# Where the first batch's x, its stage-A result and the expert weights live, and in which order they are asked for

## The chip, the cores and the metric

The kernel runs on one core of a Trainium2 chip. Its metric is the device time of one execution in microseconds (us). Engines are named as in the profile: PE is TensorE (PEld its weight loads), DVE is VectorE, ACT is ScalarE, POOL is GpSimd, SP is SyncE.

## What is computed

A Fourier layer and a layer of maxima over three products, on x of 8 batches x 3072 positions x 256 features:

```python
X = np.fft.rfft(x, axis=1)
Yr = Xr @ w_r - Xi @ w_i + b_r
Yi = Xr @ w_i + Xi @ w_r + b_i
Yr = np.sign(Yr) * np.maximum(np.abs(Yr) - 0.01, 0.0)      # Yi likewise
y = np.fft.irfft(Yr + 1j * Yi, n=3072, axis=1)
h = np.maximum(np.maximum(y @ w1, y @ w2), y @ w3)         # 256 -> 768
out = h @ w_out                                            # 768 -> 256
```

w1, w2, w3 and w_out come as 64-bit floats; the kernel reads their bits and makes two 16-bit parts of each.

## The kernel before

**Stages.** The transform of 3072 = 48 x 64 positions is done in two steps. Stage A (`stage_a`, TensorE line L408) multiplies eight chunks q of x by a table of 48 rows, copies the result (tile `pa`) out of PSUM on ScalarE (L410, two copies for each q, tiles `aq` or `zq`) and writes it to DRAM as `a_d` (L412, two DMAs, issued by ScalarE). Stages B, W and Q run over twelve k: `load_a` reads `a_d` back with other rows (tile `aj`; a k needs rows of all eight q), `stage_b` is the second step of the transform (`px`), `stage_w` the products with w_r and w_i (`py`), the bias and the soft threshold on VectorE (tile `uf`, lines L487, L548, L549), `finish_w` a maximum (L627), `stage_q` the first step of the inverse transform (`pz`), whose result goes to DRAM as `z_d`. Then `load_z` and `split_z` bring it back as two 16-bit halves `zh` (ScalarE) and `zl` (VectorE, L128), `inverse` does its second step (`pi`), and `up` and `down` are the expert network: for each of 8 column groups c and 6 slices f of 128 hidden features, 18 matmuls into `pu` and 9 into `pd`.

**Batches.** Batch 0 runs its transform alone, in 32-bit floats, ahead of everything. From then on the network of batch b runs with the transform of batch b + 1 in between: a sorted list `events` gives each step of that transform a place among the slots (c, f), and `run_until` calls what is due.

**Weights.** Eighteen parts of the expert weights (twelve of w1 to w3, 384 wide, and six of w_out, 256 wide) are loaded into tiles `rw` (14 buffers of tag `raw`), their largest value is taken (L276), and when all of a kind are there `scale` makes an exponent of it, with a small matmul `pt` (L199) between two reductions. `phases` then prepares a part in three steps, `exponent`, `combine` and `finish`, on VectorE and ScalarE; `pump` starts one part and moves those under way on by one step. `finish` writes the parts' halves into `wuh`, `wul`, `woh`, `wol`. The small weights w_r and w_i (tiles `wst`) are used as they are for batch 0 and split by `split_fft_weights`, called at f = 2 of the first column group.

**Order.** The instructions are not issued as written: a scheduler orders each engine's queue ahead of the run by place in the program and by when it expects an instruction's inputs, so that a later step may stand ahead of an earlier one on its engine. Within an engine the order is then fixed. `tc.issue_after(ins)` puts all that its block issues on the engine of `ins` behind `ins`.

**Places.** x of batch 0 goes alternately into tile `xq` (two buffers) and into tiles of tag `raw`; `aj` into two tags with two and three buffers; both are used again as soon as they have been read. x of batch 1, chunks 0 and 1 (q = 8 and 9) is loaded into `xq` during stages B to Q; their maxima (`mxx`, L394) are taken in `split_x`, ahead of `load_z`.

The start of the program's order of loads, which the change rewrites:

```python
    for q in range(3):
        load_x(q)
    for q in range(NCH):
        if q + 3 < NCH:
            load_x(q + 3)
        if q == 4:
            nc.sync.dma_start(out=id_sb, in_=ident)
            load_first_blocks(0)
            fft_weights = load_fft_weights()
        split_x(q)
        stage_a(q)
        if q in (5, 6, 7):
            load_units(w_up, up_units, 1)
```

## Time and profile before

| | |
|---|---|
| median of 3 runs | 2086.02 us (2083.11 to 2086.16) |
| profiled execution, its own time | 2082.1 us |
| its span | 2080.3 us |
| busy share of the span | PE 97%, PEld 67%, DVE 72%, ACT 47%, POOL 3% |
| mean granted clock of TensorE | 0.986 |
| moved by DMA | 165.16 MB, 79 GB/s on the mean |

The span runs from the first to the last instruction of the profile; the 1.8 us between it and the execution's own time lie around it. A busy TensorE is not one at its peak, since the ends of matmuls are modelled. The granted clock is 1.00 at 2.4 GHz and 0.50 at 1.2 GHz. Where the text speaks of a wait, the profile has inferred from semaphores what ended it.

### The profile page before, as it was taken

How to read it: one execution, taken by the hardware profiler on the slowest of the kernel's cores; microseconds unless marked ns; L12 is line 12 of the kernel's file. 1: busy time of each engine (PE TensorE's matmuls, PEld its weight loads, DVE VectorE, ACT ScalarE, POOL GpSimd, SP SyncE). 2: the span in 40 equal slices, each digit the busy share in tenths (PEclk: the TensorE clock that was granted, in tenths of full speed). 3: DMA queues.
4: the chain of work that ended last, by engine and by line, in shares of the span. 5: the costliest groups of instructions: out<-in, count | busy, mean ns of one | idle time of the engine just before them, and what ended most of it. 6: DMA issues, size and time to landing. Idle time of an engine off the chain costs nothing.

```text
span 2080.3 us, 39054 instructions
## 1 busy us (share of the span) xinstructions
PE 2022.4 (97%) x15603; PEld 1390.5 (67%) x15603; DVE 1494.4 (72%) x2951; ACT 967.9 (47%) x1929; POOL 71.2 (3%) x119
## 2 busy tenths in 40 slices
PE   5979999999999999999999999999999999999998
PEld 3746666676766666666676676666666677776666
DVE  1897888588866778668876688767887578865543
ACT  2355554455544545445554454444554445533333
POOL 0001000000000000000000000000000000000000
PEclk7989999999999999999999999999999999999999
DMA  8635231322213222132222232132221212111110
GB/s 270 191 97 154 71 90 59 100 72 77 72 57 103 74 85 67 59 99 80 74 65 83 75 89 72 59 100 72 82 77 52 72 56 67 41 42 37 33 29 23
DMA packets 116583, 165.16 MB, mean 79 GB/s; under 512 B 13137, under 2 KB 88914, under 8 KB 116306
## 3 DMA queue, kind: packets, MB, share of 16 engines
q1 hardware_dynamic: 54450, 87.15, 15.0%
q10 hardware_dynamic: 61952, 75.52, 11.8%
q8 instruction: 122, 2.00, 0.4%
q14 instruction: 59, 0.48, 0.1%
HBM read 87.13 MB, written 75.50 MB: 78 GB/s over the span
## 4 chain that ended last, share of the span: by engine, by line
PE 85%; DVE 7%; DMA 3%; ACT 2%; issue 2%; ACTq 0%; SPq 0%; POOL 0%; DVEq 0%; POOLq 0%
PE pu L133 17%; PE pu L135 17%; PE pu L134 17%; PE pd L135 6%; PE pd L133 6%; PE pd L134 5%; PE pa L408 3%; PE py L135 2%; PE py L134 2%; PE py L133 2%; DMA xq<-in_x_dram 2%; DVE u L591 1%; PE pi L133 1%; PE pi L135 1%; PE pi L134 1%
## 5 line engine op out<-in xcount | busy, mean ns | idle before, releaser
L133 PE MATMUL pu<-yh,wuh 128*128 128x384 f16 x2304 | 753.5, 327 | 0.4 <-ACT c L723 0.2
L134 PE MATMUL pu<-yl,wuh 128*128 128x384 f16 x2304 | 753.3, 327 | 0.0
L135 PE MATMUL pu<-yh,wul 128*128 128x384 f16 x2304 | 752.9, 327 | 0.0
L127 ACT ACTIVATE hh<-h 128x384 f16<-128x384 f32 x384 | 200.3, 522 | 516.2 <-DVE h L726 501.9
L724 DVE TENSOR_TENSOR c<-pu,c 128x384 f32<-128x384 f32 x384 | 212.8, 554 | 172.8 <-PE pu L135 102.5
L133 PEld LDWEIGHTS <-wuh 128*128 128x128 f16 x2304 | 225.9, 98 | 164.0 <-issue 35.5
L135 PEld LDWEIGHTS <-wul 128*128 128x128 f16 x2304 | 225.9, 98 | 149.1 <-issue 1.9
L135 PE MATMUL pd<-woh,hh 128*128 128x256 f16 x1152 | 313.4, 273 | 0.7 <-DVE hh L128 0.5
L133 PE MATMUL pd<-woh,hh 128*128 128x256 f16 x1152 | 313.8, 273 | 0.3 <-ACT hh L127 0.3
L134 PEld LDWEIGHTS <-wuh 128*128 128x128 f16 x2304 | 226.0, 98 | 131.5 <-issue 2.4
L134 PE MATMUL pd<-wol,hh 128*128 128x256 f16 x1152 | 313.7, 273 | 0.0
L128 DVE SCALAR_TENSOR_TENSOR hh<-h,hh 128x384 f16<-128x384 f32 x384 | 213.5, 556 | 115.9 <-ACT hh L127 111.8
L726 DVE TENSOR_TENSOR h<-pu,c 128x384 f32<-128x384 f32 x384 | 212.7, 554 | 47.4 <-PE pu L135 35.4
L723 ACT ACTIVATE c<-pu 128x384 f32<-128x384 f32 x384 | 186.2, 485 | 104.2 <-PE pu L135 98.2
L591 DVE SCALAR_TENSOR_TENSOR u<-py,s1x,cs 64x256 f32<-64x256 f32 x308 | 148.7, 483 | 44.9 <-ACT cs L602 40.1
L133 PE MATMUL py<-wch,tt 128*128 128x256 f16 x504 | 137.4, 273 | 0.0
L135 PE MATMUL py<-wch,tt 128*128 128x256 f16 x504 | 137.4, 273 | 0.0
L134 PE MATMUL py<-wcl,tt 128*128 128x256 f16 x504 | 137.4, 273 | 0.0
L133 PEld LDWEIGHTS <-hh 128*128 128x128 f16 x1152 | 112.7, 98 | 35.4 <-ACT hh L127 1.4
L134 PEld LDWEIGHTS <-hh 128*128 128x128 f16 x1152 | 112.7, 98 | 33.4
L135 PEld LDWEIGHTS <-hh 128*128 128x128 f16 x1152 | 112.7, 98 | 17.7 <-DVE hh L128 3.2
L749 ACT ACTIVATE o<-pd,s1u 128x256 f32<-128x256 f32 x192 | 83.2, 467 | 87.7 <-PE pd L135 42.2
(167 smaller groups left out, 2678.9 us busy)
## 6 DMA issues: line engine op xcount, KB each, us to landing
aj<-a_d SPq DMA_DIRECT2D x96, 256.0 KB, 2.9
z_d<-zs ACTq DMA_DIRECT2D x96, 256.0 KB, 2.2
zq<-z_d SPq DMA_DIRECT2D x128, 192.0 KB, 3.1
out_dram<-o ACTq DMA_DIRECT2D x192, 128.0 KB, 2.3
a_d<-aq ACTq DMA_DIRECT2D x124, 192.0 KB, 3.4
xq<-in_x_dram SPq DMA_DIRECT2D x120, 192.0 KB, 3.6
rw<-in_moe_w_dram SPq DMA_DIRECT2D x12, 384.0 KB, 6.8
xr<-in_x_dram SPq DMA_DIRECT2D x16, 96.0 KB, 3.8
```

Source lines behind the costliest of these rows:

```text
L127: nc.scalar.activation(out=hi, in_=src, func=AF.Copy, scale=scale)
L128: nc.vector.scalar_tensor_tensor(out=lo, in0=src, scalar=scale, in1=h, op0=ALU.mult, op1=ALU.subtract)
L133: nc.tensor.matmul(o, lh, rh, start=start, stop=False, **kw)
L134: nc.tensor.matmul(o, lh, rl, start=False, stop=False, **kw)
L135: nc.tensor.matmul(o, ll, rh, start=False, stop=stop, **kw)
L408: nc.tensor.matmul(pa[r][64 * c:64 * c + 64], fr[rows], xs[c][rows], start=True, stop=True)
L591: nc.vector.scalar_tensor_tensor(out=u[64 * c:64 * c + 64, j], in0=pk[r], scalar=inv[r], in1=c1[r], op0=ALU.mult, op1=ALU.add,)
L723: nc.scalar.activation(out=c1, in_=pu[0], func=AF.Copy)
L724: nc.vector.tensor_tensor(out=c1, in0=pu[1], in1=c1, op=ALU.max)
L726: nc.vector.tensor_tensor(out=h32, in0=pu[2], in1=c1, op=ALU.max)
L749: nc.scalar.activation(out=o, in_=pd[t], func=AF.Copy, scale=st[b, "su"][1])
```

## The change

- **Loads of x.** All eight chunks of batch 0's x are asked for first, with ten DMAs (two for chunk 0, two for chunk 1, then two for each pair of chunks); the identity, the first block of tables and the small weights are issued behind the last of them.
- **Places.** One tile `w_all` takes, one after the other, chunks 2 to 7 of x, all twelve `aj`, and the sixteen-bit halves of all expert weights.
- **Copies of stage A.** For batch 0 the second copy of each chunk goes to VectorE.
- **Loads of expert weights.** None during stage A; six are issued behind the third `aj`, the others as before by k.
- **Weight parts.** The subtraction and the addition in `finish` go from VectorE to GpSimd.
- **Behind stage Q.** `load_z` of batch 0 comes ahead of stage A of batch 1's chunks 0 and 1; their maxima, and the work of VectorE in `split_fft_weights`, are issued behind `zl`.

```diff
     def split_scaled(hi, lo, src, scale):
-        nc.vector.scalar_tensor_tensor(
+        return nc.vector.scalar_tensor_tensor(
...
-    wuh = const.tile([P, 3, KD, FF], F16, name="wuh")
-    wul = const.tile([P, 3, KD, FF], F16, name="wul")
-    woh = const.tile([P, NF, D], F16, name="woh")
-    wol = const.tile([P, NF, D], F16, name="wol")
+    HALF = FF // 2
+    w_all = const.tile([P, 2 * NJP * 2 * D], F16, name="w_all")
+    wup = w_all[:, 0:12 * FF].rearrange("p (v s i k w) -> p v s i k w", v=2, s=2, i=3, k=KD)
+    wdn = w_all[:, 12 * FF:].rearrange("p (f s d) -> p f s d", f=NF, s=2)
+    x_first = w_all.bitcast(F32).rearrange("p (q c w) -> p q c w", c=2, w=2 * D)
+    aj_first = w_all.bitcast(F32).rearrange("p (k d) -> p k d", d=D)
...
             def finish():
                 nc.scalar.activation(out=hi, in_=m, func=AF.Copy)
-                nc.vector.tensor_tensor(out=m, in0=m, in1=hi, op=ALU.subtract)
-                nc.vector.tensor_tensor(out=lo, in0=m, in1=r, op=ALU.add)
+                nc.gpsimd.tensor_tensor(out=m, in0=m, in1=hi, op=ALU.subtract)
+                nc.gpsimd.tensor_tensor(out=lo, in0=m, in1=r, op=ALU.add)
...
-    def load_x(q):
+    def load_x(q, count=1):
...
-            if q < NCH and q % 2:
-                pairs = [raw_tile("xr")[0:XR, 0:2 * D] for _ in range(2)]
-                for c, t in enumerate(pairs):
-                    for r in range(2):
-                        nc.sync.dma_start(out=t[64 * r:64 * r + N1], in_=xv[r, :, c])
+            if 2 <= q < NCH:
+                xq = x_first[:, q - 2:q - 2 + count]
             else:
-                xq = fft.tile([P, 2, 2 * D], F32, name="xq", bufs=2)
+                xq = fft.tile([P, 1, 2, 2 * D], F32, name="xq", bufs=2)
                 if b:
                     nc.gpsimd.memset(xq[32:64], 0.0)
-                for r in range(2):
-                    nc.sync.dma_start(out=xq[64 * r:64 * r + N1], in_=xv[r])
-                pairs = [xq[0:XR, c] for c in range(2)]
-        st["x", q] = pairs
+            for r in range(2):
+                dma = nc.sync.dma_start(
+                    out=xq[64 * r:64 * r + N1].rearrange("p q c w -> p (q c) w"),
+                    in_=xv[r, :, q4:q4 + count].rearrange("p q c w -> p (q c) w"),
+                )
+        if b == 0:
+            st["ld"] = dma
...
-    def split_x(q):
+    def largest_x(q):
...
         for r in range(2):
-            nc.scalar.activation(out=aq[:, r * 512:r * 512 + 512], in_=pa[r][0:XR], func=AF.Copy)
+            o = aq[:, r * 512:r * 512 + 512]
+            if b or r == 0:
+                nc.scalar.activation(out=o, in_=pa[r][0:XR], func=AF.Copy)
+            else:
+                nc.vector.tensor_copy(out=o, in_=pa[r][0:XR])
...
     def load_a(k):
-        first = ("vl", 3) if k < NJP and k % 5 > 1 else ("aj", 2)
-        st["a", k] = aj = fft.tile([P, 2, D], F32, name="aj", tag=first[0], bufs=first[1])
+        if k < NJP:
+            aj = aj_first[:, 2 * k:2 * k + 2]
+        else:
+            aj = fft.tile([P, 2, D], F32, name="aj", bufs=2)
+        st["a", k] = aj
...
-    for q in range(3):
-        load_x(q)
+    for q, count in ((0, 1), (1, 1), (2, 2), (4, 2), (6, 2)):
+        load_x(q, count)
+    with tc.issue_after(st["ld"].ins):
+        load_first_blocks(0)
+        fft_weights = load_fft_weights()
+        nc.sync.dma_start(out=id_sb, in_=ident)
     for q in range(NCH):
-        if q + 3 < NCH:
-            load_x(q + 3)
-        if q == 4:
-            nc.sync.dma_start(out=id_sb, in_=ident)
-            load_first_blocks(0)
-            fft_weights = load_fft_weights()
-        split_x(q)
         stage_a(q)
-        if q in (5, 6, 7):
-            load_units(w_up, up_units, 1)
-    for k in range(-3, NJP + 1):
+    for k in range(3):
+        load_a(k)
+    with tc.issue_after(st["ld"].ins):
+        load_units(w_up, up_units, 6)
+    for k in range(-1, NJP + 1):
         for fn, i in (
-            (load_a, k + 3), (stage_b, k + 1), (stage_w, k), (finish_w, k), (stage_q, k - 1),
+            (load_a, k + 4), (stage_b, k + 1), (stage_w, k), (finish_w, k), (stage_q, k - 1),
...
+    load_z(0, 0)
     for q in (NCH, NCH + 1):
-        split_x(q)
         stage_a(q)
-    load_z(0, 0)
     split_z(0)
     y = inverse(0, 0)
+    with tc.issue_after(st["zl"].ins):
+        for q in (NCH, NCH + 1):
+            largest_x(q)
...
                     if f == 2:
-                        split_fft_weights(fft_weights)
+                        with tc.issue_after(st["zl"].ins):
+                            split_fft_weights(fft_weights)
```

## Rows read from the trace of the kernel before

**Rows 1.** Busy time of every engine in four stretches of the span: up to the first px, from there to the last pz, from there to the first pu, and the rest (columns: stretch in us from the span's start; its length; busy us and count of instructions for PE, PEld, DVE, ACT and POOL; mean granted clock of TensorE; busy share of the DMA engines; GB/s).

```profile
0.00:39.54 39.54, 17.70 (x65) 6.15 (x65) 5.15 (x11) 10.59 (x18) 2.08 (x6) 0.71 0.80 238
39.54:114.30 74.76, 69.22 (x328) 55.00 (x328) 61.06 (x147) 27.89 (x57) 0.55 (x3) 0.95 0.65 206
114.30:128.50 14.20, 6.74 (x40) 3.67 (x40) 12.58 (x40) 6.39 (x11) 1.88 (x2) 0.55 0.66 167
128.50:2080.30 1951.80, 1928.70 (x15178) 1325.66 (x15175) 1415.61 (x2757) 923.01 (x1843) 66.66 (x108) 1.00 0.24 71
```

**Rows 2.** The chain of work that ended last, followed back and put in order of time, from 13 to 40 us (columns: start, duration, what).

```profile
19.46 4.96 DMA mb_all<-in_dft_ib_dram
...
26.86 5.83 DMA rw<-in_moe_w_dram
...
32.72 3.83 DMA a_d<-aq
...
36.62 2.87 DMA aj<-a_d
```

**Rows 3.** ScalarE and its queue of issued DMAs (ACTq) in order of time, 13 to 34 us (columns: start, duration, engine, line, operation, tiles, shapes, count; in brackets the idle time before it and what ended it).

```profile
26.04 0.88 ACTq L412 DMA_DIRECT2D a_d<-zq  x2
26.97 1.08 ACT L410 ACTIVATE aq<-pa 112x512 f32<-112x512 f32 x2 [4.60 <-DMA wst<-in_w_i_dram]
29.14 1.52 ACTq L412 DMA_DIRECT2D a_d<-aq  x2
30.71 0.60 ACT L410 ACTIVATE aq<-pa 112x512 f32<-112x512 f32 x1 [2.65 <-DMA qf<-in_dft_ib_dram]
```

**Rows 4.** Four short stretches, with the columns of rows 1; the last two figures of each line, DMA share and GB/s, are what is read here.

```profile
4.00:8.00 4.00, 3.48 (x14) 1.73 (x18) 0.00 (x0) 0.49 (x1) 0.00 (x0) 1.00 1.03 223
12.00:14.00 2.00, 2.00 (x11) 0.57 (x8) 0.00 (x0) 0.93 (x2) 0.54 (x1) 1.00 0.94 337
24.00:28.00 4.00, 0.00 (x0) 0.00 (x0) 2.03 (x4) 1.03 (x2) 0.00 (x0) 0.50 0.47 161
44.00:54.00 10.00, 10.00 (x47) 8.91 (x47) 4.89 (x9) 1.74 (x4) 0.00 (x0) 0.82 1.05 402
```

**Rows 5.** The same chain of work in order of time, from 0 to 60 us: three steps of TensorE at full clock.

```profile
49.67 0.43 PE py L483 x2
50.10 0.89 PE px L456 x8
...
54.01 0.86 PE pz L495 x2
```

**Rows 6.** The stretch from 58 to 114 us, with the columns of rows 1.

```profile
58.00:114.00 56.00, 51.17 (x250) 40.04 (x248) 51.27 (x128) 23.81 (x48) 0.55 (x3) 1.00 0.54 155
```

**Rows 7.** The same chain in order of time, from 94 to 129 us.

```profile
96.50 1.86 DVE mxx L394 x3
...
98.68 0.59 DVE mxx L394
...
105.31 0.34 DVE wol L324
...
112.47 0.61 DVE uf L549
...
116.42 4.94 DMA xq<-in_x_dram
121.49 0.69 DVE mxx L394
...
122.91 0.47 DVE rw L323
...
125.06 0.59 DVE mxx L394
125.65 1.20 DVE zl L128
```

**Rows 8.** All engines in order of time, 117 to 123.5 us, with the columns of rows 3: the load of zq (SPq, the queue of SyncE) and the first instruction that reads it.

```profile
117.51 1.34 SPq L683 DMA_DIRECT2D zq<-z_d  x2
...
122.96 1.15 ACT L127 ACTIVATE zh<-zq,s0u 96x1024 f16<-96x1024 f32 x1 [1.58 <-DMA zq<-z_d]
```

**Rows 9.** What TensorE's matmuls waited for between 39.6 and 128.5 us (columns: engine and line, what it waited for, us in total, times, longest).

```profile
PE px L456 <- DMA aj<-a_d: 16.1, 1, 16.1
...
PE pt L199 <- DVE col L197: 2.7, 2, 2.2
PE pz L498 <- DVE uf L549: 2.3, 1, 2.3
```

**Rows 10.** VectorE's groups of instructions between 58 and 114 us, one for each line and shape (columns: line, engine, operation, tiles, shapes, count; busy us, mean ns of one; idle time before them).

```profile
L549 DVE TENSOR_TENSOR uf<-uf,t 128x512 f32<-128x512 f32 x10 | 6.8, 685 | 0.0
...
L323 DVE TENSOR_TENSOR rw<-rw,wuh 128x384 f32<-128x384 f32 x6 | 3.3, 551 | 0.0
...
L323 DVE TENSOR_TENSOR rw<-rw,woh 128x256 f32<-128x256 f32 x3 | 1.3, 418 | 0.0
```

**Rows 11.** GpSimd's groups over the whole span, with the columns of rows 10.

```profile
L532 POOL TENSOR_SCALAR tt<-tt 128x256 f16<-128x256 f16 x14 | 10.3, 736 | 314.0 <-ACT tt L127 255.3 <-DVE hh L128 58.6
L540 POOL COPY ts<-tt 128x256 f16<-128x256 f16 x14 | 5.5, 396 | 0.9
```

**Rows 12.** DMA issues by tile over the whole span (columns: tiles, queue, operation, count, KB each, median us from issue to landing).

```profile
zq<-z_d SPq DMA_DIRECT2D x128, 192.0 KB, 3.1
```

More of the change, by code (lines that the diff above doesn't have):

```diff
@@ L329, in fourier_maxout_kernel @@
     out_v2 = w_out.bitcast(U32)
-    HALF = FF // 2
     w_up = Weights("u", [
-        (wuh[:, i, kd, v:v + HALF], wul[:, i, kd, v:v + HALF],
-         up_v[i][kd * P:(kd + 1) * P, 2 * v:2 * v + 2 * HALF])
-        for v in range(0, FF, HALF) for i in range(3) for kd in range(KD)
+        (wup[:, v, 0, i, kd], wup[:, v, 1, i, kd],
+         up_v[i][kd * P:(kd + 1) * P, 2 * v * HALF:2 * (v + 1) * HALF])
+        for v in range(2) for i in range(3) for kd in range(KD)
     ])
     w_dn = Weights("d", [
-        (woh[:, f], wol[:, f], out_v2[f * P:(f + 1) * P]) for f in range(NF)
+        (wdn[:, f, 0], wdn[:, f, 1], out_v2[f * P:(f + 1) * P]) for f in range(NF)
     ])
@@ L368, in rows_of @@
         return v[2 * k:2 * k + 2].rearrange("j p d -> p j d")
[L371 removed]
+    def load_x(q, count=1):
         b, q4 = divmod(q, NCH)
[L373 removed]
+        xv = x[b].rearrange("(n1 q c r n) d -> r n1 q c (n d)", n1=N1, c=2, r=2, n=2)
         with tc.issue_after(st["ld"].ins) if q >= NCH + 2 else nullcontext():
[L375 to L379 removed]
+            if 2 <= q < NCH:
+                xq = x_first[:, q - 2:q - 2 + count]
             else:
[L381 removed]
+                xq = fft.tile([P, 1, 2, 2 * D], F32, name="xq", bufs=2)
                 if b:
                     nc.gpsimd.memset(xq[32:64], 0.0)
[L384 to L398 removed]
+            for r in range(2):
[5 more added lines that the diff above has]
+            st["ld"] = dma
+        for i in range(count):
+            st["x", q + i] = [xq[0:XR, i, c] for c in range(2)]
+    def largest_x(q):
+        b, q4 = divmod(q, NCH)
+        for i, xp in enumerate(st["x", q]):
+            nc.vector.tensor_reduce(
+                out=batch(b, "x")[0:XR, 2 * q4 + i:2 * q4 + i + 1], in_=xp, axis=AX.X,
+                op=ALU.max, apply_absolute_value=True,
+            )
     def stage_a(q):
@@ L409, in stage_a @@
         for r in range(2):
-            nc.scalar.activation(out=aq[:, r * 512:r * 512 + 512], in_=pa[r][0:XR], func=AF.Copy)
+            o = aq[:, r * 512:r * 512 + 512]
[3 more added lines that the diff above has]
+                nc.vector.tensor_copy(out=o, in_=pa[r][0:XR])
         for c in range(2):
+            n0 = 8 * q4 + 4 * c
             nc.scalar.dma_start(
-                out=batch(b, "a")[:, 8 * q4 + 4 * c:8 * q4 + 4 * c + 4, :],
+                out=batch(b, "a")[:, n0:n0 + 4, :],
                 in_=aq[64 * c:64 * c + N1].rearrange("p (n d) -> p n d", n=NQ),
@@ L691, in split_z @@
         zl = fft.tile([96, NQ, D], F16, name="zl", bufs=1)
-        split_scaled(*(t.rearrange("p n d -> p (n d)") for t in (zh, zl)), st["zq"], st[b, "su"][0][0:96])
+        st["zl"] = split_scaled(
+            *(t.rearrange("p n d -> p (n d)") for t in (zh, zl)), st["zq"], st[b, "su"][0][0:96]
+        )
         st["z"] = zh, zl
@@ L717, in up @@
                 mm3(
-                    p[:, 0:NT], wuh[:, i, kd, f * P:(f + 1) * P], wul[:, i, kd, f * P:(f + 1) * P],
-                    y[0][:, kd], y[1][:, kd], start=kd == 0, stop=kd == KD - 1,
+                    p[:, 0:NT],
+                    *(wup[:, f // 3, s, i, kd, f % 3 * P:f % 3 * P + P] for s in range(2)), y[0][:, kd], y[1][:, kd], start=kd == 0, stop=kd == KD - 1,
                 )
@@ L742, in down @@
             mm3(
-                pd[t], lh, ll, woh[:, f], wol[:, f], start=f == 0 and t != 1,
+                pd[t], lh, ll, wdn[:, f, 0], wdn[:, f, 1], start=f == 0 and t != 1,
                 stop=f == NF - 1 and t != 0, skip_group_check=t < 2,
@@ L795, in fourier_maxout_kernel @@
         with tc.issue_after(st["ld"].ins):
-            if k in (-2, 1, 4):
-                load_first_blocks(k // 3 + 2)
+            if k in (-1, 1, 4):
+                load_first_blocks((k + 5) // 3)
             load_units(w_up, up_units, 2)
```

15 lines of the change are left out of this document (2 added, 13 removed).

## The prediction, made before the changed kernel ran

> **What bounds the kernel now.** I read the busy time by stages first [rows 1]. The last 1951.8 us, from the first matmul of the expert network on, keep TensorE busy for 1928.7 us at full clock; nothing in the diff takes matmuls out of that stretch, so what the change can move lies in the 128.5 us ahead of it. There the rows show three stages. Until 39.54 us TensorE works for 17.7 us only: x comes in, stage A runs, its result goes to DRAM. Then 74.76 us of the first batch's stages B, W and Q. Then 14.2 us from the last pz to the first pu, with TensorE busy for 6.74 us and a mean clock of 0.55.
>
> In the first stage I followed the chain [rows 2]. Behind the x loads it runs over the first table (4.96 us), over the first expert weights rw (5.83 us), to the last write of a_d (3.83 us) and the first load of aj (2.87 us). The ScalarE rows [rows 3] show why loads of tables stand on a path of writes: the write of a_d issued at 26.04 and the copies behind it start only when a wst load has landed (4.60 us idle), the next when qf has (2.65 us idle). Those copies read neither tile, so it is the writes' issue that waits for earlier transfers of the other queue, and it holds ScalarE's copies up behind it. The transfers [rows 4]: x alone moves 223 GB/s with the queues full (1.03), x and a_d together 337, and from 24 to 28 us there is a hole (share 0.47).
>
> In the second stage the reader is to see that TensorE has no time to give until late. Per k the chain has 0.89 us for px, sixteen py in pairs of 0.43, and 0.86 for pz [rows 5], so 5.2 us, times 12 is 62 us. Until about 96 us that is back to back. VectorE is busy for 51.27 of 56 us there [rows 6] and falls behind at the end: four maxima of batch 1's x (1.86 + 0.59 us) stand in its queue at 96.5, and the last uf reaches TensorE at 113.1 [rows 7].
>
> In the third stage [rows 7, 8] zq is asked for at 117.51, zh starts at 122.96, but zl not before 125.65, since two maxima that wait for a late xq (4.94 us) stand ahead of it.
>
> **The change part by part.** The base is the profiled execution, 2082.1 us with a span of 2080.3.
>
> *x first, tables behind, copies on two engines.* 24 DMAs for batch 0's x become 10, none waits for a buffer any more, and the bytes are the same. Eight chunks of 393 kB are 3.15 MB; at 223 GB/s 14.1 us. As much again for a_d, at 337 GB/s or more, is 9.3 us at most; twelve tables (1.3 MB) at the same rate take 4 us. That is 27.4 us of a full queue from 2 us on, so the last a_d can't land before about 27 to 29 us (before: 36.55, where the aj load starts). Three rw loads (1.2 MB, 3.5 us) that stood ahead of the last writes now stand behind three aj loads. So the bound from below is 28 + 2.87 = 31, a gain of 8.5. From above: the twelve tables are now asked for directly behind x, while the writes of a_d still wait for earlier transfers of the other queue, now bigger ones. If the second a_d waits for the last x (about 18 us), seven chunks are left; each has about 0.6 us of copy on ScalarE and two writes issued (0.88 to 1.52 us for two [rows 3]), 1.5 to 2.1 us, together 10.5 to 15, and 3.8 to land: 32 to 37, the gain is between 4.5 and nothing. The half of the copies that goes to VectorE costs about 0.6 us each (as on ScalarE) while VectorE is idle, and shortens this chain. I take 31.5, so first px at 34.5: **5 us gained** (0 to 8.5). At half clock TensorE starts into stage B as before, so that ramp neither costs nor pays.
>
> *aj kept in the weights' place.* TensorE waits for no aj once stage B runs (the one wait, 16.1 us, is the first px) [rows 9], so more buffers are worth nothing there. Their price is that weight parts may be written only when the px that read that place are over; the parts are finished several k later, and I put it at nothing. SP issues aj, rw and tables in the old order but for three aj in front; TensorE takes its fourth aj three px and two times sixteen py after the first, 9.6 us, and 3.3 MB lie ahead of it, 8.3 us at the 400 GB/s that aj and rw bring from 44 us on [rows 4]: covered by 1.3 us, and by more while the clock is at half.
>
> *GpSimd finishes the weight parts.* Two VectorE instructions per part leave. Start to start they cost 0.47 us (384 wide) and 0.34 us (256 wide) [rows 7], so nine parts (six and three [rows 10]) give back 6 x 0.94 + 3 x 0.68 = 7.7 us of the 51.27, and the moved maxima another 2.45. What GpSimd needs for two inputs no row shows. Its copy of 256 elements takes 396 ns, its scalar form 736 [rows 11]; two copies' worth would be 0.8, so for 384 elements between 0.6 and 1.2 us; I take 1.1 (the scalar form's rate) and 0.74 for 256. Nine parts are 17.6 us on an idle engine. If that hid completely, TensorE would get back at most its waits behind VectorE [rows 9]: 2.7 for pt and 2.3 for pz, 5 us. If GpSimd and VectorE exclude each other, VectorE's 41.1 us grow by up to 17.6 to 58.7, which is 7.4 more than today. Between these, with half of it colliding, VectorE has 50 us, and the maxima are away from the place where they cost most: **2 us gained** (-7.4 to 5).
>
> Here a page speaks against the change. The Trainium skill, "SBUF — State Buffer", section "Who interferes with whom", has the two engines share one port pair as an exclusive lock: a VectorE instruction with two SBUF inputs, or in a two-port mode, and a GpSimd instruction that reads SBUF wait for each other in full. No row here shows it: GpSimd's rows before are copies, fills and a scalar form. By the rule the sum would go to its lower end, as far as L309, L316, L317 and L549 (two SBUF inputs each, as L549's row shows [rows 10]) meet GpSimd.
>
> *z ahead of batch 1's x.* zl then waits for zh and zq alone. zq was asked for at 117.51 and its median landing is 3.1 us [rows 12], against some 5 here beside xq and a_d. With zq at 121, zl ends at 122.3 instead of 126.85. A write of a_d still runs beside it, and one GpSimd instruction may be in the way: **4 us gained** (2 to 5). Late is then x of chunk 10, which waits for the maxima behind zl; its matmuls have slot 3 among the events, three f later, so that is hidden.
>
> *The start of the network.* The split of the small weights also moves behind zl: its reduces and its four pt matmuls ran in idle gaps and now run among the first pu. Nine more parts on GpSimd have to be done by the fourth f, three f of 1951.8/384 = 5.1 us on: 17.6 us of GpSimd against 15, begun before. I count **0.5 us lost** (-1 to 4).
>
> Sum: 5 + 2 + 4 - 0.5 = 10.5 us. Span 2069.8, own time 2071.6. The median of the runs stands 3.9 us above the profiled execution (2086.02), so I forecast **2075.5 us**. About 0.2%, 4 us, is what a measurement can tell from no change.
>
> **The rivals.** *Tables in the way*: stage A ends as late as now, because tables and writes wait for each other as [rows 3] show, only earlier placed. Then 0 to 1 instead of 5: 2080. For it speaks that table loads aren't taken away, against it that rw is.
>
> *The port*, the one on the other side: every GpSimd instruction holds VectorE up. Stages B to Q take 7.4 us more instead of 2 less, and the second nine parts hold VectorE, full at that point, up by another 17.6 - 7.7 = 10 us, of which TensorE's reserve takes perhaps half. 5 + 4 - 7.4 - 5 = -3.4, so 2089, and 2083 to 2092 with the gains' own bounds. It decides once the net hold in both stretches passes some 9 us.
>
> *Everything hides*: stage A ends at its transfer bound (8.5), TensorE's waits behind VectorE go (4.5), zl 4.5: 17.5 gained, 2068.5.
>
> **How the numbers follow.** Forecast 0.47; everything hides 0.17; tables 0.17; the port 0.19, half of it near no change, half slower. Faster: 0.47 + 0.17 + most of the tables' case (0.13) = 0.77; the same 0.04 + 0.09 = 0.13; slower 0.10. The range holds the first three and the near half of the port: 2065 to 2086.
>
> **What would show it.** The first px between 31 and 37 us; copies of stage A without waits for wst or qf; TensorE without a wait for VectorE's col around the dn maxima; VectorE's two-input instructions longer than 0.55 us or with gaps beside GpSimd's if the port rules; zl right behind zh; first pu near 118 us, and from there 1952 us as now. Wrong it would be if the stretch behind the first pu grew, or if TensorE waited within stages B to Q.

## The result and the profile after

The changed kernel takes 2095.69 us (median of 4 runs, 2094.10 to 2097.70), the kernel before 2085.56 (4 runs); the ratio is 1.0051, 95% interval 1.0034 to 1.0069. By the medians that is 10.1 us slower where 10.5 us faster was forecast, and outside the range. The profiled execution took 2096.82 us with a span of 2095.0.

The same four stretches as in [rows 1], of the changed kernel:

```profile
0.00:40.21 40.21, 21.49 (x64) 5.52 (x65) 5.53 (x8) 6.36 (x10) 2.09 (x6) 1.00 0.85 204
40.21:124.43 84.22, 72.57 (x327) 57.44 (x328) 63.70 (x139) 29.19 (x60) 23.18 (x25) 0.93 0.61 197
124.43:136.83 12.40, 6.82 (x35) 3.04 (x36) 8.23 (x26) 5.92 (x10) 3.97 (x5) 0.50 0.47 133
136.83:2095.00 1958.17, 1930.36 (x15179) 1326.37 (x15177) 1417.72 (x2752) 921.39 (x1841) 76.39 (x120) 1.00 0.25 71
```

Against [rows 1] the first stretch is 0.7 us longer, the second 9.5, the third 1.8 shorter, the last 6.4 longer: 14.7 us of span, some more than the medians show. In the second stretch TensorE is busy for 72.57 us instead of 69.22, so 6.1 of the 9.5 us are idle time and 3.4 are matmuls that took longer, at a mean granted clock of 0.93 against 0.95. The 1.00 in the first row is no reading: the trace of this run has no record of the clock before 45.1 us.

**Stage A.** The chain of the changed kernel from 9 to 41 us, in order of time:

```profile
9.82 0.37 ACTq L417
...
10.23 7.41 DMA a_d<-aq
...
18.17 6.91 DMA a_d<-zq
...
28.87 3.79 DMA bias<-in_b_i_dram
...
33.51 3.75 DMA a_d<-aq
...
37.34 2.73 DMA w_all<-a_d
```

A write of a_d issued into the burst of x takes 7.41 us to land, the next on the chain 6.91; [rows 2] has 3.83 for one. SyncE's queue tells the other half:

```profile
3.06 15.36 SPq L383 DMA_DIRECT2D w_all<-in_x_dram  x6
18.47 0.94 SPq L767 DMA_DIRECT2D mb_all<-in_dft_ib_dram  x1
```

The six loads of x behind the first four are not all issued by 6 us; it takes until 18.4, the tables follow at 18.5, and the small weights at 25. Their places are free, and they read no a_d; what their issue waited for (SyncE, 0 to 42 us; us in total, times, longest) is all the same

```profile
SPq L383 <- DMA a_d<-aq: 9.8, 2, 9.2
```

In the trace the DMAs of SyncE and ScalarE take eight completion semaphores in turn, and none is issued before the one that had its semaphore last has landed: the load of x issued at 17.26 us follows the landing of ScalarE's first write of a_d at 17.24. What ScalarE waited for meanwhile (8 to 41 us), and the last of these waits in order of time:

```profile
...
ACT aq L412 <- DMA a_d<-aq: 4.9, 1, 4.9
ACT aq L412 <- DMA a_d<-zq: 4.3, 1, 4.3
ACT zq L412 <- DMA a_d<-zq: 4.2, 1, 4.2
```

```profile
26.96 3.02 ACTq L417 DMA_DIRECT2D a_d<-zq  x2
30.07 1.08 ACT L412 ACTIVATE aq<-pa 112x512 f32<-112x512 f32 x2 [4.30 <-DMA a_d<-zq]
```

The copies' waits for wst and qf of [rows 3] are gone, and 13.4 us of waits for a write of a_d stand in their place. In 9.1 of them a copy needs the buffer (two aq, one zq) whose write is still on its way. In the other 4.3 an aq is named as held up by a write of zq, which frees no aq: there the copy stands in ScalarE's queue behind the issue of zq's two writes, which takes 3.02 us because the second waits for an earlier write to land.

**Stages B to Q.** VectorE's and GpSimd's groups in the changed kernel (columns as [rows 10]; VectorE from 58 to 125 us, GpSimd from 50 to 200 us):

```profile
L555 DVE TENSOR_TENSOR uf<-uf,t 128x512 f32<-128x512 f32 x10 | 7.6, 755 | 0.0
L311 DVE SCALAR_TENSOR_TENSOR xl<-rw,xl 128x384 uint32<-128x384 uint32 x9 | 7.0, 779 | 0.8 <-ACT xl L307 0.8
L633 DVE TENSOR_REDUCE mxu<-uf 128x1 f32<-128x512 f32 x10 | 6.8, 677 | 0.0
...
L278 DVE TENSOR_REDUCE mwd<-rw 128x1 f32<-128x256 f32 x6 | 2.5, 417 | 8.3 <-DMA rw<-in_moe_w_out_dram 8.3
```

```profile
L325 POOL TENSOR_TENSOR rw<-rw,w_all 128x384 f32<-128x384 f32 x12 | 13.4, 1113 | 89.1 <-DMA w_all<-a_d 57.5 <-ACT w_all L324 31.5
L326 POOL TENSOR_TENSOR w_all<-rw 128x384 f16<-128x384 f32 x12 | 10.8, 899 | 1.9 <-PE px L462 1.1
```

L555 is L549 of [rows 10], 685 ns there, and L311 is this line of the kernel before (58 to 125 us):

```profile
L309 DVE SCALAR_TENSOR_TENSOR xl<-rw,xl 128x384 uint32<-128x384 uint32 x9 | 5.0, 552 | 0.7 <-ACT xl L305 0.7
```

The maxima mwd (L278) wait 8.3 us for loads of w_out; the raw buffers these need are freed by GpSimd's finish, and each of the six loads is issued within 0.1 us behind the end of an L326. That this makes the whole wait is not shown: with the finish on GpSimd alone (e2) it is 1.0 us. The reader sees the longer instructions one by one where the two engines meet (start, duration):

```profile
116.71 0.67 DVE L633 TENSOR_REDUCE mxu<-uf 128x1 f32<-128x512 f32 x1
117.31 1.24 DVE L311 SCALAR_TENSOR_TENSOR xl<-rw,xl 128x384 uint32<-128x384 uint32 x1
...
121.04 0.55 DVE L319 SCALAR_TENSOR_TENSOR rw<-rw,xl 128x384 f32<-128x384 uint32 x1
121.51 1.40 DVE L555 TENSOR_TENSOR uf<-uf,t 128x512 f32<-128x512 f32 x1
```

```profile
117.22 0.91 POOL L325 TENSOR_TENSOR rw<-rw,w_all 128x384 f32<-128x384 f32 x1
118.21 1.02 POOL L326 TENSOR_TENSOR w_all<-rw 128x384 f16<-128x384 f32 x1
121.45 0.91 POOL L325 TENSOR_TENSOR rw<-rw,w_all 128x384 f32<-128x384 f32 x1 [2.23 <-ACT w_all L324]
```

L311 beside L325 takes 1.24 us and L555 beside the next 1.40, each about its own time plus most of GpSimd's; L319, with GpSimd idle until near its end, 0.55.

**Behind the first pu.** The first eight f of the network (up to the start of the ninth hh on ScalarE), first in the kernel before and then in the changed one, and two stretches of the latter (columns as [rows 1]):

```profile
128.50:178.80 50.30, 49.60 (x308) 25.85 (x306) 43.50 (x107) 27.08 (x56) 5.71 (x6) 0.96 0.41 119
136.60:195.30 58.70, 53.47 (x312) 26.90 (x311) 46.17 (x103) 25.69 (x54) 15.57 (x19) 0.88 0.43 115
145.00:165.00 20.00, 14.91 (x91) 8.00 (x93) 20.00 (x56) 10.21 (x22) 7.10 (x9) 0.99 0.08 20
164.60:174.80 10.20, 10.20 (x30) 2.94 (x27) 7.84 (x17) 4.05 (x9) 1.89 (x2) 0.50 0.58 155
```

From 145 to 165 us VectorE is busy without a gap and TensorE for 14.9 of 20 us: the network starts on a VectorE that has a backlog. Behind that TensorE runs at 1.2 GHz for 10 us; the kernel before, where it stood for 0.7 us in all, stays at 2.4 GHz there. So the backlog is paid twice: of the 8.4 us that the first eight f grew by, 4.5 are idle time of TensorE, and 3.9 are matmuls, about as many, that took longer.

### The profile page after: what moved, and what is told of

It reads as the page before. It is cut to its first block, busy times and chain, and to the rows that moved or that the text cites. A ratio compares the mean times of both kernels' runs of the same rounds, so it can differ in the third digit from the quotient of the medians.

```text
span 2095.0 us, 39066 instructions
## 1 busy us (share of the span) xinstructions
PE 2031.2 (97%) x15603; PEld 1392.4 (66%) x15603; DVE 1495.2 (71%) x2923; ACT 962.9 (46%) x1921; POOL 105.6 (5%) x155
## 3 DMA queue, kind: packets, MB, share of 16 engines
q1 hardware_dynamic: 54226, 87.15, 15.5%
## 4 chain that ended last, share of the span: by engine, by line
PE 87%; DVE 5%; DMA 3%; ACT 2%; issue 2%; POOL 0%; ACTq 0%; SPq 0%; DVEq 0%; POOLq 0%
PE pu L133 17%; PE pu L135 17%; PE pu L134 17%; PE pd L135 6%; PE pd L133 6%; PE pd L134 6%; PE pa L408 3%; PE py L133 2%; PE py L135 2%; PE py L134 2%; DMA xq<-in_x_dram 2%; PE pi L133 1%; DVE u L597 1%; PE pi L135 1%; PE pi L134 1%
## 5 line engine op out<-in xcount | busy, mean ns | idle before, releaser
L133 PE MATMUL pu<-yh,w_all 128*128 128x384 f16 x2304 | 753.3, 327 | 1.7 <-DVE c L732 1.5
L134 PE MATMUL pu<-yl,w_all 128*128 128x384 f16 x2304 | 752.8, 327 | 0.0
L135 PE MATMUL pu<-yh,w_all 128*128 128x384 f16 x2304 | 752.6, 327 | 0.0
L133 PEld LDWEIGHTS <-w_all 128*128 128x128 f16 x2304 | 225.8, 98 | 164.7 <-issue 35.9
L135 PEld LDWEIGHTS <-w_all 128*128 128x128 f16 x2304 | 225.9, 98 | 149.1 <-issue 1.7
L135 PE MATMUL pd<-w_all,hh 128*128 128x256 f16 x1152 | 313.7, 273 | 1.7 <-DVE hh L128 1.6
L133 PE MATMUL pd<-w_all,hh 128*128 128x256 f16 x1152 | 314.2, 273 | 0.8 <-ACT hh L127 0.8
L134 PEld LDWEIGHTS <-w_all 128*128 128x128 f16 x2304 | 226.0, 98 | 132.9 <-issue 3.9
L134 PE MATMUL pd<-w_all,hh 128*128 128x256 f16 x1152 | 314.2, 273 | 0.0
L757 ACT ACTIVATE o<-pd,s1u 128x256 f32<-128x256 f32 x192 | 83.3, 467 | 89.8 <-PE pd L135 44.7
```

The source lines that it names most:

```text
L133: nc.tensor.matmul(o, lh, rh, start=start, stop=False, **kw)
L134: nc.tensor.matmul(o, lh, rl, start=False, stop=False, **kw)
L135: nc.tensor.matmul(o, ll, rh, start=False, stop=stop, **kw)
L757: nc.scalar.activation(out=o, in_=pd[t], func=AF.Copy, scale=st[b, "su"][1])
```

## The experiments

All times are compared with runs of the kernel before on the same chip. The lengths of stretches are from each kernel's profiled execution: start of the first px; from there to the start of batch 0's last pz; from there to the first pu; from there to the start of the ninth hh (the first eight f); the rest. A profiled execution varies by itself: eight kernels with the stage A of before have their first px between 37.4 and 40.3 us, six with its stages B to Q (before, e3, e5, e6, e13, e17) reach the last pz 73.0 to 75.6 us later, and eight with its start of the network (before, e4, e7, e9, e10, e11, e17, e18) need 49.1 to 50.7 us for the first eight f. A difference within these spans shows nothing. The profiled executions of e4, e5, e7 and e11 were 2.7, 6.3, 3.4 and 2.9 us above their medians, that of e9 3.3 below.

| kernel | ratio to before, 95% | first px | to last pz | to first pu | first eight f | rest |
|---|---|---|---|---|---|---|
| before | 1 | 39.5 | 74.4 | 14.6 | 50.3 | 1901.5 |
| changed | 1.0051 (1.0034 to 1.0069) | 40.2 | 83.6 | 12.8 | 58.7 | 1899.7 |
| e1 loads and z | 1.0074 (1.0062 to 1.0086) | 39.2 | 80.7 | 12.6 | 63.2 | 1901.9 |
| e2 GpSimd alone | 1.0038 (1.0026 to 1.0050) | 38.8 | 83.1 | 18.1 | 48.1 | 1900.5 |
| e3 z alone | 1.0047 (1.0035 to 1.0059) | 38.9 | 73.6 | 12.1 | 64.6 | 1903.2 |
| e4 loads alone | 1.0025 (1.0014 to 1.0036) | 40.7 | 80.1 | 14.8 | 50.5 | 1903.2 |
| e5 z, split free | 1.0000 (0.9991 to 1.0009) | 40.3 | 74.8 | 12.4 | 57.7 | 1901.5 |
| e6 split late | 1.0044 (1.0031 to 1.0057) | 39.8 | 75.6 | 15.4 | 58.3 | 1902.3 |
| e7 e4, 4 zs | 1.0015 (1.0006 to 1.0024) | 39.7 | 78.2 | 15.3 | 50.7 | 1902.7 |
| e8 idle GpSimd | 1.0044 (1.0032 to 1.0057) | 38.9 | 77.2 | 14.6 | 57.6 | 1900.9 |
| e9 e7, 4 aq | 0.9995 (0.9986 to 1.0004) | 36.7 | 74.7 | 15.1 | 49.8 | 1897.6 |
| e10 e7, x in 8 | 1.0010 (1.0001 to 1.0019) | 39.3 | 75.1 | 14.0 | 50.7 | 1900.9 |
| e11 e9, tables late | 1.0015 (1.0006 to 1.0024) | 35.8 | 80.8 | 15.4 | 49.1 | 1902.5 |
| e12 GpSimd, half | 1.0003 (0.9994 to 1.0012) | 37.4 | 72.8 | 14.5 | 51.3 | 1900.6 |
| e13 batch 1 later | 1.0014 (1.0004 to 1.0023) | 38.5 | 73.0 | 16.3 | 41.2 | 1914.3 |
| e14 changed, later | 1.0070 (1.0058 to 1.0082) | 39.8 | 80.7 | 12.8 | 47.4 | 1912.5 |
| e15 e9, x8, z, later | 1.0027 (1.0016 to 1.0039) | 38.2 | 76.2 | 13.1 | 44.7 | 1911.6 |
| e16 e15 without z | 1.0025 (1.0013 to 1.0037) | 38.1 | 76.0 | 17.2 | 40.7 | 1914.3 |
| e17 before, 4 aq | 1.0003 (0.9992 to 1.0015) | 38.2 | 73.0 | 15.3 | 50.1 | 1904.6 |
| e18 e9, zq first | 1.0004 (0.9993 to 1.0014) | 37.6 | 74.9 | 15.5 | 50.5 | 1903.4 |

**The change taken apart, e1 to e4.** The first theory after the result was that GpSimd's finish alone is to blame (G).

e1: the changed kernel with the finish on VectorE.

```diff
-                nc.gpsimd.tensor_tensor(out=m, in0=m, in1=hi, op=ALU.subtract)
-                nc.gpsimd.tensor_tensor(out=lo, in0=m, in1=r, op=ALU.add)
+                nc.vector.tensor_tensor(out=m, in0=m, in1=hi, op=ALU.subtract)
+                nc.vector.tensor_tensor(out=lo, in0=m, in1=r, op=ALU.add)
```

> The changed kernel with the two instructions that finish a weight part given back to VectorE; loads, places and z stay changed. Theory G (GpSimd's finish is what costs: it stretches VectorE's instructions and frees the raw buffers late): the 9.4 us that the stretch from first to last pz grew by and the 6.4 us behind the first pu both go, 2095.7 - 15.8 = 2080. Rival P (the places: parts that wait until aj and x have left them): it stays within 3 us of 2095.7. Rival Z (the weights' split pushed behind the first pu by the z move): the 6.4 us stay, the 9.4 go, 2086.

2098.05 us against 2081.96. It is not faster than the changed kernel, so G, by which GpSimd alone is to blame, falls.

e2: the kernel before with those two lines the other way round.

> The kernel before with the finish on GpSimd and nothing else. Theory G: 2085.6 plus 12 to 16, 2098 to 2102. Rival P or Z: between 2083 and 2087, since VectorE has less to do and nothing else is touched.

2090.18 us, 8 us lost: 8.7 to the last pz, 3.5 to the first pu, and 2.2 won back in the first eight f. Both theories missed: G wanted 12 to 16, the others no loss.

e3: the kernel before with z loaded first, the maxima and the split behind zl.

```diff
+    load_z(0, 0)
     for q in (NCH, NCH + 1):
         split_x(q)
         stage_a(q)
-    load_z(0, 0)
     split_z(0)
     y = inverse(0, 0)
+    with tc.issue_after(st["zl"].ins):
+        for q in (NCH, NCH + 1):
+            largest_x(q)
...
-                        split_fft_weights(fft_weights)
+                        with tc.issue_after(st["zl"].ins):
+                            split_fft_weights(fft_weights)
```

> The kernel before with z loaded first and the two maxima and the weights' split behind zl, and nothing else. Theory G: the stretch from last pz to first pu shrinks by 1.8 us (as in the changed kernel) to 4 us (as forecast), the rest as before: 2081.5 to 2084. Rival Z: the network loses 3 to 6 us: 2086 to 2090.

2092.23 us. The z stage is 2.5 us shorter, the first eight f 14.3 longer: more than rival Z had put there.

e4: e1 without the z part.

> The loads and places alone: x asked for first, x and aj kept in the weights' place, tables behind x, half of the first batch's copies on VectorE; the finish on VectorE and z as before. Theory G: stage A 0.7 us later as in the changed kernel, nothing else: 2085 to 2087. Rival P: 2092 to 2096. If the forecast's 5 us are merely hidden by GpSimd's trouble: 2081.

2088.49 us, between the times of G and P: 5.7 us lost between the first px and the last pz, the stretch that rival P means, though not for its reason (e7). Each of the three parts is slower by itself: 0.25% for loads and places, 0.47% for z, 0.38% for GpSimd. Loads and z add up (0.72% against e1's 0.74%). With GpSimd all three come to 0.51% instead of 1.1%: beside the other two its finish doesn't cost 8 us more. By the ratios it gives 5 back, but the intervals of e1 and the changed kernel overlap, so that it gives anything is not shown. The first eight f show some of it: 63.2 in e1, 58.7 in the changed kernel. Why the three add up to so little was not tried.

**The split behind zl, e5 and e6.** e5 is e3 with the split taken up whenever it can be; e6 is the kernel before with nothing but the split held behind zl.

```diff
                     if f == 2:
-                        split_fft_weights(fft_weights)
+                        with tc.issue_after(st["zl"].ins):
+                            split_fft_weights(fft_weights)
```

> z alone as in e3, but the split of the small weights may again be taken up before zl. Theory S (the split, held behind zl, is what fills VectorE in the first f of the network): the first eight f come back from 64.6 to about 50 us, the 2.5 us of the z stage stay won: 2078 to 2080 against 2082 before. Rival M (VectorE's backlog, maxima and weight parts, is merely moved from the idle z stage into the network, whatever is named): 2088 to 2092, no better than e3.

> The kernel before with the split of the small weights held behind zl; z and the maxima stay where they were. Theory S: the first eight f take 8 to 14 us longer: 2088 to 2094. Rival M: 2081 to 2084, since the order of z and the maxima is untouched.

e5 took 2082.22 us, e6 2091.90. So z and the maxima without the split cost nothing and bring nothing, neither the 2 to 4 us of theory S nor the loss of rival M; the split held late is 9 us by itself, and it is what e3 lost by. Where it went is in the maxima of the small weights, of the kernel before and of e6 (count, min/median/max ns, first and last start in us):

```profile
L233 DVE TENSOR_REDUCE mxc<-wst x2: 686/686/687, 25.3 to 26.3; 128x1 f32<-128x512 f32 x2
```

```profile
L233 DVE TENSOR_REDUCE mxc<-wst x2: 678/679/680, 150.5 to 151.9; 128x1 f32<-128x512 f32 x2
L243 DVE TENSOR_TENSOR wst<-wst x2: 414/414/415, 152.5 to 152.9; 128x256 f32<-128x256 f32 x2
```

In the kernel before they ran at 25 us (the maximum of the bias at 34.4, ql at 36.1), on a VectorE that had nothing to do in stage A. Behind zl they run at 150 us, on the engine that TensorE waits for there; two mxc, two subtractions, the maximum of the bias and ql are 3.3 us. Busy times of e6 (columns as [rows 1]) and the longest wait of its ScalarE from 136 to 160 us:

```profile
136.00:144.00 8.00, 5.92 (x39) 3.62 (x37) 8.00 (x22) 4.58 (x9) 0.00 (x0) 1.00 0.01 3
144.00:152.00 8.00, 6.93 (x43) 3.85 (x42) 7.97 (x23) 2.80 (x7) 0.00 (x0) 1.00 0.00 0
152.00:160.00 8.00, 6.36 (x40) 3.15 (x41) 8.00 (x31) 3.49 (x9) 0.95 (x1) 1.00 0.18 49
```

```profile
ACT wch L127 <- DVE sc L215: 4.5, 1, 4.5
```

VectorE is full, and ScalarE stands for 4.5 us at wch, up to 156.9, for the scale that comes out of the late maxima; in the kernel before its longest wait for the split there is 0.6 us. Work and wait are not a sum, since ScalarE waits while VectorE does that work. Nor are they the whole 8.0 us that the first eight f grew by: TensorE lacks 2.1 us from 136 to 144 already, ahead of the first late maximum, where the kernel before lacks 0.7:

```profile
136.00:144.00 8.00, 7.30 (x44) 3.82 (x42) 8.00 (x24) 4.57 (x9) 0.00 (x0) 1.00 0.00 0
```

Holding the split also changed the order in which VectorE took the weight parts; what that costs was not tried apart. Nearly all of e6's growth is idle time of TensorE (7.8 us against 0.7, busy for 50.5 against 49.6). In e3, which grew by 14.3, it is 9.4 us of idle time, and 55.2 us busy at a mean granted clock of 0.84.

**Stage A and the loads, e7 and e9 to e11.** ScalarE in e4 (columns as [rows 3]):

```profile
64.79 0.38 ACTq L653 DMA_DIRECT2D z_d<-zs  x1
...
68.94 0.60 ACT L307 ACTIVATE xl<-xh,bwu 128x384 uint32<-128x384 uint32 x1
74.48 0.60 ACT L652 ACTIVATE zs<-pz 128x512 f32<-128x512 f32 x1 [4.94 <-DMA z_d<-zs]
...
75.58 0.54 ACT L324 ACTIVATE w_all<-rw 128x384 f16<-128x384 f32 x1 [0.50 <-ACT zs L652]
```

With no buffer to wait for, four aj and the table ga_sb are asked for between 61 and 64 us, and one write of z_d, issued at 64.79, lands 9.6 us later. ScalarE stands for its zs buffer, and the weight part behind it waits too. e7 gives zs four buffers.

```diff
-        zs = fft.tile([P, 2, D], F32, name="zs")
+        zs = fft.tile([P, 2, D], F32, name="zs", bufs=4)
```

> e4 with four buffers for zs instead of two, so that ScalarE's copy need not wait for a late write of z_d. Theory Q (aj no longer waits for a buffer, so more loads stand in the queues; one z_d write takes 9.6 us beside them, ScalarE stands for 4.9 us at zs, and the weight parts behind it come late): the stretch from first px to last pz goes from 80.1 back to 75 to 76, the time to 2083 to 2085. Rival P (weight parts wait until x and aj have left their place): 80 us and 2088 stay.

2084.94 us, as expected, but the stretch to the last pz came down to 78.2 only, 1.9 us where 4 to 5 were expected. That is less than such stretches vary, and e7's profiled execution was a long one: e10, whose program is the same from the first px on, has 75.1. ScalarE's wait for z_d is gone; what theory Q is worth lies between these. e9 has four aq as well:

```diff
-        return fft.tile([XR, NQ * D], F32, name=name, bufs=1 if name == "zq" else 2)
+        return fft.tile([XR, NQ * D], F32, name=name, bufs=1 if name == "zq" else 4)
```

> e7 with four buffers for aq instead of two. Theory buffers (stage A's copies wait for the write of the chunk that had the buffer before: 4.44, 4.17 and 4.25 us in e7, since a write beside the burst of x takes 7 us to land): most of these waits go, the first px comes at 32 to 36 instead of 39.7 us, the time is 2079 to 2082. Rival queue (the transfers themselves are the limit): the first px stays at 38 to 40, 2084 to 2086.

2079.03 us against 2079.11 before. The intervals of e9 and e7 don't meet. The first px is 3.0 us earlier than in e7, at 36.7 where 32 to 36 was expected, and the stretch to the last pz back at 74.7. The five kernels with x first and two aq have their first px at 39.2 to 40.7 (changed, e1, e4, e7, e14), e18 with e9's stage A at 37.6, so 2 to 3 us of this are the buffers'. That makes their theory right in its result; but ScalarE still waits for writes (8 to 34 us):

```profile
ACT aq L412 <- DMA a_d<-zq: 10.9, 2, 6.9
...
ACT zq L412 <- DMA a_d<-zq: 0.4, 1, 0.4
```

11.3 us of waits are left of e7's 12.9, 6.9 of them ahead of the last two chunks. But for 0.4 us they are not for buffers, since a write of zq frees no aq: the copies stand in ScalarE's queue behind the issue of writes, as above. How the buffers bring their gain is thus not shown in full.

e10, x in eight DMAs instead of ten:

```diff
-    for q, count in ((0, 1), (1, 1), (2, 2), (4, 2), (6, 2)):
+    for q, count in ((0, 1), (1, 1), (2, 3), (5, 3)):
```

> e7 with batch 0's x in eight DMAs (1, 1, 3 and 3 chunks) instead of ten. Theory lanes (the last two x loads are issued at 17.15 and 18.07 us only, because each waits for a write of a_d that was issued in its turn before it): all x is asked for by 8 us, the stall of SP's queue is gone, the first px comes at 36 to 38, 2081 to 2084. Rival buffers: x was not what the copies waited for, and the writes behind a longer burst land later still: first px 39 to 42, 2084 to 2087.

2081.81 us against 2079.11, so not clearly faster than e7 by the ratios. All x is asked for by 11.8 instead of 18.4 us, and the first px moves by 0.4: the late issues of x are not what stage A waits for.

e11, the small tables behind three aj:

```diff
         load_first_blocks(0)
-        fft_weights = load_fft_weights()
-        nc.sync.dma_start(out=id_sb, in_=ident)
...
+    with tc.issue_after(st["ld"].ins):
+        fft_weights = load_fft_weights()
+        nc.sync.dma_start(out=id_sb, in_=ident)
```

> e9 with the small weights, the bias, qf and the identity asked for behind the first three aj instead of behind x. If tables still stand in the way of the writes (the writes of chunks 5 to 7 wait for bias and qf between 26 and 34 us in e7), the first px comes 1 to 4 us earlier than in e9 and the time falls by as much; the price is that the bias and qf come late for the first uf and pz, at most 2 us. If not: as e9 within 1 us.

2082.45 us. Stage A ends 0.9 us earlier, less than it varies, and 6 us are lost behind it, more than the price expected, and ScalarE's row names it (36 to 60 us):

```profile
ACT tf L467 <- DMA wst<-in_w_i_dram: 11.2, 1, 11.2
```

e17 gives the kernel before four aq and nothing else.

> The kernel before with four buffers for aq instead of two, and nothing else. If the three microseconds that e9 won in stage A are the buffers' alone, the first px comes 2 to 3 us earlier here too and the time is 2 to 4 us below before. If they need x asked for first (in the kernel before the copies lose 7.3 us to issues that wait for tables and some 4 us to buffers): the first px moves by less than 1 us and the time stays within 2 us of before.

2081.43 us against 2080.82: no change. So the buffers are worth something only to x asked for first, and x asked for first is worth nothing measurable over the kernel before even with them.

**GpSimd and VectorE, e8 and e12.** e8 leaves VectorE's work alone and adds two GpSimd instructions for each part whose result nobody reads.

```diff
                 nc.vector.tensor_tensor(out=lo, in0=m, in1=r, op=ALU.add)
+                s = fft.tile([P, 384], F32, name="scratch", bufs=1)[:, 0:width]
+                nc.gpsimd.tensor_tensor(out=s, in0=hi, in1=hi, op=ALU.subtract)
+                nc.gpsimd.tensor_tensor(out=s, in0=s, in1=s, op=ALU.add)
```

> The kernel before, VectorE's finish untouched, and beside it two GpSimd two-input instructions per part on a scratch tile whose result nobody reads: work added, none taken. Theory port (GpSimd and VectorE hold each other up): VectorE's two-input instructions stretch, the stretch from first px to last pz grows by half or more of e2's 8.7 us, and the time is 2086 to 2092. Rival late (what costs in e2 is that GpSimd finishes a part later and so frees raw buffers later): nothing is stretched, 2081 to 2084.

2090.95 us, 9 us lost by work that feeds nothing. One row each of the kernel before, of e2 and of e8 (VectorE, 58 to 125 us):

```profile
L302 DVE TENSOR_SCALAR xh<-rw 128x384 uint32<-128x384 uint32 x9 | 3.1, 353 | 0.0
```

```profile
L302 DVE TENSOR_SCALAR xh<-rw 128x384 uint32<-128x384 uint32 x9 | 6.2, 699 | 0.0
...
L627 DVE TENSOR_REDUCE mxu<-uf 128x1 f32<-128x512 f32 x10 | 6.7, 674 | 0.0
```

```profile
L302 DVE TENSOR_SCALAR xh<-rw 128x384 uint32<-128x384 uint32 x9 | 4.2, 474 | 0.0
...
L323 DVE TENSOR_TENSOR rw<-rw,wuh 128x384 f32<-128x384 f32 x7 | 5.0, 715 | 0.0
```

The same L302 takes 353, 699 and 474 ns, L323 715 where [rows 10] has 551, and the reduce stays at 674. So GpSimd's work beside VectorE is a cost by itself, as the port theory said, and rival late, by which nothing is stretched, falls. Its size by stretch was off: 2.8 us to the last pz, less than half of e2's 8.7, and 7.3 in the first eight f, of which 3.4 are idle time of TensorE and 3.9 longer busy time at a mean granted clock of 0.88. What the other part of e2's loss is stays open. TensorE waits 4.7 us there at one pt for the maxima of w_out (2.2 before, [rows 9]), but in e8, where VectorE itself finishes the parts, it waits 4.8 us at the same place; only e2 also waits 3.1 us for uf at the wide pz, 0.2 before.

e12: GpSimd finishes the second half of each weight's parts only.

```diff
+                e = nc.vector if n < len(self.parts) // 2 else nc.gpsimd
+                e.tensor_tensor(out=m, in0=m, in1=hi, op=ALU.subtract)
+                e.tensor_tensor(out=lo, in0=m, in1=r, op=ALU.add)
```

> The kernel before with GpSimd finishing only the second half of the parts of each weight (up 6 to 11, dn 3 to 5), most of them in the network's first six f, where e2 won 2.2 us. Theory port, paid where VectorE is on the path: first px to last pz as before within 2 us (74 to 76), the first eight f 46 to 50 us, the time 2079 to 2083. Rival: GpSimd costs wherever it runs beside a full VectorE: first eight f 52 us or more, 2085 to 2089.

2079.62 us against 2079.11: nothing lost and nothing won; the stretch to the last pz is untouched, as expected, but the first eight f don't shrink.

**Room behind zl, e13 to e16 and e18.** If VectorE's backlog is what everything is paid with, starting batch 1 later should pay.

```diff
-        p = i if b == 1 else (b - 2) * SLOTS + NF * i + 2
+        p = i + 4 if b == 1 else (b - 2) * SLOTS + NF * i + 2
...
-            p = 8 + 2.2 * (k + 2) if b == 1 else (b - 1) * SLOTS + 2.8 * (k + 2)
+            p = 12 + 1.9 * (k + 2) if b == 1 else (b - 1) * SLOTS + 2.8 * (k + 2)
...
+                if (b, c, f) == (0, 1, 0):
+                    split_fft_weights(fft_weights)
```

> The kernel before with batch 1's x, stages B to Q and the split of the small weights taken up four f later in the network (and 1.9 instead of 2.2 f apart, so that they end where they ended). Theory N (VectorE has a backlog in the first f, each piece of work put there is paid by TensorE): the first eight f take 43 to 47 us instead of 50, the kernel is 3 to 6 us faster than before. Rival D (the work is only given back by the denser schedule of batch 1): the first eight f are shorter, the next forty longer by as much, within 2 us of before.

2083.76 us against 2081.80. The first eight f shrink by 9.1 us, and the rest grows by 12.8: rival D. Two stretches of the kernel before and of e13 show it: TensorE does 27 more matmuls in the first 40 us and 55 fewer in the next 200.

```profile
128.00:168.00 40.00, 39.30 (x237) 20.16 (x235) 37.55 (x96) 22.20 (x45) 3.82 (x4) 0.94 0.30 86
168.00:368.00 200.00, 197.75 (x1574) 134.81 (x1573) 161.50 (x313) 101.55 (x204) 10.89 (x17) 0.99 0.31 91
```

```profile
128.00:168.00 40.00, 39.72 (x264) 24.32 (x263) 35.32 (x92) 21.72 (x45) 1.90 (x2) 0.93 0.21 57
168.00:368.00 200.00, 194.69 (x1519) 128.82 (x1518) 157.91 (x308) 99.26 (x199) 13.03 (x19) 0.98 0.33 95
```

> The changed kernel with that same later start of batch 1 and of the split. Theory N: the 8.4 us that its first eight f lost go, 58.7 to 46 to 50 us, and it comes to within 3 us of before; the 9 us of first px to last pz stay. Rival D: it stays 8 us or more behind before.

e14, the changed kernel with the same edit, which also lets the split go from behind zl: 2096.15 us against 2081.80. Its first eight f come down from 58.7 to 47.4, and 12.8 us come back behind them.

> e9 with x in eight DMAs, z ahead of batch 1's maxima as in the change, and the later start of batch 1 and of the split; the finish is on VectorE. Theory N: z's 2.5 us are no longer given back in the network, stage A keeps its 3 us: 6 to 12 us faster than before. Rival D: within 3 us of before.

> e15 with z and the maxima in their old order. Theory N: 1.5 to 4 us slower than e15, which is what z ahead is worth once VectorE has room behind it. If z's gain is given back in any case: as e15 within 1 us.

e15 took 2086.93 us, e16 (no z) 2088.11, both slower than before, where theory N had e15 6 to 12 us faster; their ratios are the same within their intervals. In e15's profiled execution the way from the last pz to the first pu is 4.1 us shorter and the first eight f 4.0 us longer than in e16: z's gain is given back in the very next stretch, even with room made.

e18 is e9 with only the load of z moved ahead.

> e9 with the load of z ahead of batch 1's first x, and the four maxima left where they were, ahead of zl. If the late load of zq is part of what the z stage waits for: last pz to first pu 1 to 2 us shorter than e9's 15.1, the first eight f as in e9, 1 to 3 us below before. If zl's place behind the maxima decides alone: no change against e9, within 2 us of before.

2081.30 us against 2080.82, with the z stage at 15.5: the load alone brings nothing, and only where zl also stands ahead of the maxima (e3, e5) is the stage shorter. No version here beats the kernel before; e9 beats the changed one by nearly 12 us by their ratios and equals the kernel before.

## Why the prediction was wrong

**The step that failed most** is the start of the network, put at 0.5 us lost (-1 to 4). The prediction saw that the split's reduces and pt matmuls ran in idle gaps and would run among the first pu, and then priced GpSimd's parts instead. It also began with the sentence that only the first 128.5 us can move. Measured in the first eight f: 8.4 us in the changed kernel, 14.3 for the z part alone (e3), 8.0 for the split alone (e6). Work that VectorE had done while idle made TensorE wait, and where the waits were long the clock that TensorE was granted fell too, a cost that no term of the sum has. The changed kernel itself with only the split let go was not tried.

**z ahead**, 4 us (2 to 5): 1.8 in its own stretch, 2.5 in e3. The mechanism was right and the size just under its lower bound, or inside the range (e3); but VectorE's work that used to stand ahead of zl went to an engine without a gap, and by e5 and by e15 against e16 nothing of it reaches the end.

**x first**, 5 us (0 to 8.5): nothing; the first px came at 40.21. The rival *tables in the way* had the result right, but its cause is at most a small part: a load of the bias is still on the chain with 3.79 us, yet moving the tables gives 0.9 us (e11), less than stage A varies, and four buffers for aq 2 to 3 (e9). The prediction's slow bound, 37 us, counted 0.6 us of copy, two issues per chunk and 3.8 us for the last write. It overlooked that a copy needs the buffer of a write that takes 7 us to land.

**aj kept in the weights' place**, nothing: wrong by 5.7 us with x first (e4), and this and GpSimd's term make the 9.5 us of stages B to Q, where 2 us gained were forecast. The step asked whether TensorE waits for aj, whether the weights' place is free in time and whether the fourth aj lands in time. That the loads, free of buffers, would crowd a small write of z_d out to 9.6 us, and that ScalarE and the weight parts stand behind that write, was not asked. With more buffers for zs and aq the loss is gone (e9); how much of it is this write stays open.

**GpSimd**, 2 us gained (-7.4 to 5): the instruction's cost was about right, 1.1 us estimated against 1113 and 899 ns measured for 384 elements, 0.74 against 728 and 1017 for 256. The collision was not half hidden: alone the finish costs 8 us (e2), and GpSimd work without any use 9 (e8). The rival *the port* had the mechanism, but its agreement in size is partly luck: its 7.4 us in stages B to Q is near e2's 8.7, of which the collision by itself shows 2.8 (e8), and of its 5 us for the network, near e8's 7.3, the changed kernel shows nothing, since with the finish on GpSimd its first eight f are 4.5 us shorter than e1's. The measured time lies beyond its range, up to 2092, too. By the rule cited from the Trainium skill, "SBUF — State Buffer", section "Who interferes with whom", instructions with two SBUF inputs and those in a two-port mode meet GpSimd's lock and a reduce does not. L323 and L555, with two inputs, and the reduces L627 and L633 agree. L302 has one input, so by the rule it would have to run in a two-port mode, which no row shows.

**What would have shown it** was named rightly: the stretch behind the first pu grew, and TensorE waited within stages B to Q. Not asked was what VectorE's idle time in stage A was used for.

## What to carry to other kernels

Before holding work behind something on an engine, look up where that work ran: if it sat in another stage's idle time, its whole length moves into the new place, and the waits of what depends on it with it. Here holding back 3.3 us of such work cost 9 (e6). Taking away the buffer that paces a queue of loads lets them crowd out a short write, so look for the engine that stands behind that write. An idle GpSimd isn't free for two-input work beside a full VectorE (e8); price its busy time on VectorE too.

## What the runs showed of the hardware

GpSimd work that feeds nothing lengthens VectorE's instructions beside it: L302 from 353 to 474 ns on the mean (e8); in the changed kernel a 0.68 us instruction takes 1.40 us where both start together. A 192 KB write issued into a burst of loads takes 7.4 us to land, a 256 KB one 9.6, where the medians are 3.3 us (a_d in the changed kernel) and 2.1 (z_d of batch 0 in e4). Six loads asked for in a row took SyncE 15.4 us to issue, with none of them waiting for a buffer: by the profile 9.8 us of it went by until writes of the other queue had landed. TensorE, busy for 14.9 of 20 us, was granted 1.2 GHz for the 10 us behind them.
